# Reordering a product, a routing step and two row updates at the end of an attention and mixture-of-depths kernel

## The chip, the cores and the metric

The kernel runs on one core of one Trainium2 chip. A core has a matrix engine (TensorE, PE in the profile), a vector engine (VectorE, DVE), an engine for copies and functions (ScalarE, ACT), a general engine (GpSimd, POOL), an engine that here issues transfers only (SyncE, SP) and 16 DMA engines. [...] The metric is device time in microseconds; the time of the kernel before is 681.06 us, the median of three runs that lie between 681.03 and 681.25 us.

## What is computed

Attention with pooled queries runs over 8 batches, 8 heads, 1152 keys and 64 channels. Its output, 576 rows of 512 channels a batch, goes through a mixture-of-depths layer that updates 128 rows of every batch.

```python
q_pool = q.reshape(B, H, S // 2, 2, D).mean(axis=3)
attn = softmax(q_pool @ k.transpose(0, 1, 3, 2) / sqrt(D))
x = (attn @ v), as [B, 576, 512]
for b in range(B):
    scores = x[b] @ w_gate
    top_idx = the 128 rows with the highest scores
    xe = x[b, top_idx]
    h = np.maximum(xe @ w1, 0.0)          # 512 -> 1024
    ye = h @ w2                           # 1024 -> 512
    g = 1.0 / (1.0 + np.exp(-scores[top_idx]))
    out[b, top_idx] = xe + g[:, None] * ye     # all other rows stay x
```

## The kernel before, in words

**The main loop.** `run` goes over 64 halves: 32 pairs of heads, each in two halves of 288 pooled queries. A half is scores on TensorE, exponents on ScalarE, their sums on GpSimd and VectorE, and the weighted values on TensorE. All rows of a finished batch go to the output in memory; the picked rows are later read back, updated and written over.

**The layer for picked rows.** Two batches are taken together. Both weight layers are done by a scheme with seven products of half-size blocks in place of eight: the input blocks a11, a12 (first batch) and a21, a22 (second batch), four sums s1 to s4 of them, and weight blocks b11, b21, b22 and sums t1 to t4 of the weights. The seven products are, in the numbering of `second_layer`, (a11, b11), (a12, b21), (s1, t1), (s2, t2), (s3, t3), (s4, b22), (a22, t4). Their results are added up to the blocks of the output. `product` is one of them: 16 passes of TensorE over 128 columns in the first layer (line 1434), 8 passes over 256 columns in the second (line 1444). It takes its PSUM tile from `banks`, a pool of four tiles that are handed out in rotation, so that the tile of one call has to be free of what was put into it four calls earlier.

**The ending.** Batches 4 and 5 (their second layer), and 6 and 7 (both layers), are left for `ending`, which starts when the last half has been computed. Nothing schedules here: the order of the Python calls is the order of the instructions on every engine. The layers are generators, and `pieces(unit, n)` runs one up to its n-th `yield`. The units are: `layer`, the first layer of batches 4 and 5; `second`, the products of a second layer, in a given order, one at a `next`; `third`, the first layer of batches 6 and 7; `new`, the routing of batch 7.

**Routing of batch 7** (`routed`, b = 7). VectorE counts, for each row, how many rows score higher (line 1125), and makes from the ranks five 0/1 matrices (the picks, line 1167; a `yield` follows). Five small products with these (line 1177, ten passes) give the picked rows' numbers and gates; ScalarE copies them out (1185; a `yield`). A transposition (1188) turns them into columns, ScalarE copies these (1189, 1190), and GpSimd gathers the rows with an indirect DMA into the tile named `lines` (1223; a `yield`). Later, TensorE transposes the gathered rows (1271), ScalarE copies them (1272), and they are the input of `third`'s remaining products.

**The stretch that the change touches** is this (lines 1584 to 1594). ScalarE copies the result of `third`'s first product; the rest of the ranking and the picks; the five small products and their copy; product 7 of batches 4 and 5 and its copy to y7 (1587); the transposition and the gather; what is left of `layer`, which is one addition on VectorE and the ReLU of block c21 on ScalarE (1469); the four sums of the second layer's inputs on VectorE (1521), for products 3 to 6; `third`'s second product (a12, b21) with its addition on VectorE and its ReLU on ScalarE (`hidden`, 1467); then products 3, 4 and 5 of batches 4 and 5.

**The last rows.** At the end come the seven products of batches 6 and 7 in the order 1, 7, 3, 4, 5, 6, 2. `scaled` (1448) is one VectorE operation that adds gate times a block to half of the rows of a batch. Product 5 is part of both halves of batch 7's rows, so two operations add it (1637, 1638); then GpSimd writes the rows of batch 7 (1639), and, after products 6 and 2, those of batch 6 (1642). The rows of batch 7 are in the tile `lines`, those of batch 6 in `xe`. The write of batch 6 waits until the write of batch 7 has landed.

Of the kernel before, what the change touches and what calls it, by code (L numbers as in the profile page):

```python
# [539 lines left out]
class _Plain:  # L540
# [886 lines left out]
    def product(self, layer, of, by, to):  # L1427

        n = of.shape[1]
        if layer == 1:  # L1430
            to = self.lines_of(to)[:, :, 0 : of.shape[2]]
            for f in range(by.shape[2] // P):
                for k in range(n):
                    self.nc.tensor.matmul(  # L1434
                        to[:, f, :],
                        lhsT=by[:, k, f * P : (f + 1) * P],
                        rhs=of[:, k, :],
                        start=k == 0,
                        stop=k == n - 1,
                    )  # L1440
        else:
            to = to[0 : of.shape[2], 0 : by.shape[2]]
            for k in range(n):
                self.nc.tensor.matmul(to, lhsT=of[:, k, :], rhs=by[:, k, :], start=k == 0, stop=k == n - 1)  # L1444
        return to
# [9 lines left out]
    def first_layer(self, a, s, c, m, kept=None):  # L1455

        copy = self.nc.scalar.copy
        (a11, a12, _, a22), (s1, s2, s3, s4), (c11, c12, c21, c22), (u, w) = a, s, c, m  # L1460
        b11, b21, b22 = (self.quarter(1, i, j) for i, j in ((0, 0), (1, 0), (1, 1)))
        t1, t2, t3, t4 = (self.summed(1, i) for i in range(4))

        def product(of, by):
            return self.product(1, of, by, self.banks()[:, 0, :])

        def hidden(to, x, y):
            self.add(to, x, y)
            self.nc.scalar.activation(to, to, AF.Relu)

        copy(u, product(a11, b11))
        yield
        hidden(c11, u, product(a12, b21))
        yield
        copy(w, product(s1, t1))
        yield
        self.add(u, u, product(s2, t2))
        self.add(w, w, u)
        yield
        ps = product(s3, t3)  # L1480
        hidden(c22, w, ps)
        self.add(u, u, ps)
        yield
        hidden(c12, w, product(s4, b22))
        yield
        ps = product(a22, t4)
        if kept is not None:
            copy(kept, ps)
            yield
            ps = kept  # L1490
        hidden(c21, u, ps)
        yield
# [30 lines left out]
    def ending(self, halves, old):  # L1523


        nc, half, copy, add = self.nc, self.Dm // 2, self.nc.scalar.copy, self.add
        last = halves[-1]["pair"]

        def pieces(unit, n=None):
            for i, _ in enumerate(unit):  # L1530
                if i + 1 == n:
                    break

        tokens, a, s = self.left
        w = tokens[0]["w"]
# [5 lines left out]
        layer = self.first_layer(a, s, c, m, kept)  # L1541
# [13 lines left out]
        _, new, _ = self.routing.pop()  # L1555
        pieces(old, 1)
        pieces(new, 1)
        pieces(layer, 2)
        for of in (halves[-3]["pair"], last):
            self.divided(of)  # L1560
            self.stored(of)
# [7 lines left out]
        y1, y2, y7, y3, y4 = (acc[1][0:w, i * half : (i + 1) * half] for i in range(5))  # L1569
        room = self.ffn.tile([P, 4, 512], F32, name="s", bufs=1).rearrange("p a n -> p (a n)")  # L1570
        s = self.lines_in(room, self.NFC // 2, w, 4)
        second = self.second_layer(c, s, (1, 2, 7, 3, 4, 5, 6))
# [4 lines left out]
        n = self.NFC * P  # L1577
# [4 lines left out]
        sums = self.lines_in(room[:, 2 * n :], self.ND // 2, w, 4)  # L1582
        third = self.first_layer(a, sums, of_tiles, self.lines_in(self.room[:, 6 * half :], 4, w, 2))
        pieces(third, 1)

        pieces(new, 2)
        copy(y7, next(second))
        pieces(new, 1)
        pieces(layer)
        self.four_sums(c, s)  # L1590
        pieces(third, 1)
        to = [token["xe"][0:w, i * half : (i + 1) * half] for token in tokens for i in range(2)]
        four, five = tokens
# [6 lines left out]
        ps = next(second)  # L1600
# [4 lines left out]
        ps = next(second)  # L1605
# [13 lines left out]
        six, seven = tokens = self.last_tokens  # L1619
        to = [token["xe"][0:w, i * half : (i + 1) * half] for token in tokens for i in range(2)]  # L1620
        y1, y7, y3, y4 = (self.room[0:w, i * half : (i + 1) * half] for i in range(6, 10))
# [3 lines left out]
        second = self.second_layer(of_tiles, s, (1, 7, 3, 4, 5, 6, 2))  # L1625
        copy(y1, next(second))
        self.scaled(to[0], y1, six, to[0])
        ps = next(second)
# [3 lines left out]
        self.scaled(to[2], y4, seven, to[2])  # L1632
        self.add(y3, y3, y4)
        self.scaled(to[3], y3, seven, to[3])
        self.scaled(to[1], y3, six, to[1])
        ps = next(second)
        self.scaled(to[3], ps, seven, to[3])
        self.scaled(to[2], ps, seven, to[2])
        self.written(seven, seven["index"])
        self.scaled(to[1], next(second), six, to[1])  # L1640
        self.scaled(to[0], next(second), six, to[0])
        self.written(six, six["index"])
# [190 lines left out]
```

## Time and profile before

| | us |
|---|---|
| median of three runs | 681.06 (681.03 to 681.25) |
| the profiled execution | 682.7 |
| its span, first to last instruction | 680.9 |
| TensorE busy | 671.4 (99%) |
| VectorE busy | 573.9 (84%) |
| GpSimd busy | 504.0 (74%) |
| ScalarE busy | 453.9 (67%) |
| DMA, mean over the span | 150 GB/s |

The granted TensorE clock is 0.999 of full speed. Times in the text that have two digits behind the point and lie between 600 and 681 are moments in the span of the profiled execution. In a timeline line the columns are the start, the duration from the first start to the last end, the engine, the line of the kernel, the operation, what it writes and reads, the number of instructions, and in brackets how long the engine sat idle before and what ended that. A matrix multiplication of the program appears as two passes in the profile: x16 on line 1434 is one whole product of a first layer, x8 on line 1444 one of a second layer. [...] the time until the data has landed is in the list of DMA issues.

### The profile page before, as it was taken

To read this page: it belongs to the slowest core of one execution; us is meant where nothing else is said; L and a number is where in the kernel's file an instruction comes from. 1 tells how busy PE (TensorE), PEld (TensorE's weight loads), DVE (VectorE), ACT (ScalarE), POOL (GpSimd) and SP (SyncE) were. 2 spreads that over 40 slices of the span, in tenths; PEclk is the share of its full clock that TensorE was granted. 3 is DMA by queue.
4 is the path that set the end of the run, shared out by engine and by line. 5 is a ranking of instruction groups with operands and counts; after the bars stand their busy time and mean duration, and the time that the engine had idled before them with its cause. 6 is when DMAs were issued, how large, how long until landed. Compare 5 with 4: busy or idle time off the path is not lost.

```text
span 680.9 us, 23432 instructions
## 1 busy us (share of the span) xinstructions
PE 671.4 (99%) x9954; PEld 445.8 (65%) x9954; DVE 573.9 (84%) x816; ACT 453.9 (67%) x990; POOL 504.0 (74%) x476
## 2 busy tenths in 40 slices
PE   8999999999999999999999999999999999999996
PEld 6656666665666568676666657767666665658895
DVE  3878998999999887686998987686999998798774
ACT  5677777777877773856777778483787777773220
POOL 4778888889888983866897888383889889885011
PEclk9999999999999999999999999999999999999999
DMA  8888899858886785753879688674588878735310
GB/s 165 165 180 185 199 195 198 165 104 190 193 187 125 166 164 93 205 96 75 206 150 203 125 177 161 128 179 80 118 208 188 151 159 163 173 100 134 63 41 36
DMA packets 391786, 101.99 MB, mean 150 GB/s; under 512 B 371577, under 2 KB 375545, under 8 KB 390649
## 3 DMA queue, kind: packets, MB, share of 16 engines
q1 hardware_dynamic: 390232, 96.03, 67.8%
q0 software_dynamic: 1280, 4.20, 1.9%
q8 instruction: 79, 1.29, 0.7%
q14 instruction: 35, 0.28, 0.2%
q10 hardware_dynamic: 160, 0.20, 0.1%
HBM read 82.77 MB, written 17.62 MB: 147 GB/s over the span
## 4 chain that ended last, share of the span: by engine, by line
PE 85%; DVE 7%; issue 3%; DMA 2%; POOL 1%; ACT 1%; SPq 0%; DVEq 0%; POOLq 0%; ACTq 0%
PE ps L882 38%; PE ps L900 37%; PE ps L1357 7%; DVE fold L926 2%; DVE pick L1125 2%; PE ps L1444 1%; ACT p L889 1%; DMA lines<-row_rank 1%; POOL acc L921 1%; DMA p<-in_q_dram 1%; DVE acc L1453 0%; DMA out_dram<-xe,index 0%; DMA out_dram<-lines,index 0%; DVE kT L778 0%; PE ps L1434 0%
## 5 line engine op out<-in xcount | busy, mean ns | idle before, releaser
L889 ACT ACTIVATE p<-ps 128x576 f32<-128x576 f32 x576 | 320.8, 696 | 3.0 <-PE ps L882 2.8
L921 POOL TENSOR_TENSOR acc<-p 128x576 f32<-128x576 f32 x192 | 278.7, 1479 | 29.2 <-ACT p L889 28.9
L882 PE MATMUL ps<-qT,kT 64*64 64x288 f32 x4608 | 293.0, 404 | 0.7 <-DVE token L632 0.5
L900 PE MATMUL ps<-p,v_sb 64*64 64x288 f32 x4608 | 291.3, 403 | 0.0
L882 PEld LDWEIGHTS ps<-qT,kT 64*64 64x64 f32 x4608 | 172.8, 132 | 108.5 <-ACT p L889 18.8
L900 PEld LDWEIGHTS ps<-p,v_sb 64*64 64x64 f32 x4608 | 172.6, 133 | 107.0 <-ACT p L889 14.0
L926 DVE TRANSPOSE_TENSOR_REDUCE fold<-p 128x54 f32<-128x1728 f32 x64 | 126.2, 1972 | 31.7 <-ACT p L889 31.2
L926 DVE TRANSPOSE_TENSOR_REDUCE fold<-acc 128x54 f32<-128x1728 f32 x64 | 124.6, 1947 | 10.9 <-POOL acc L921 10.6
L908 ACT COPY two<-ps 128x576 f32<-128x576 f32 x64 | 40.8, 638 | 136.5 <-PE ps L900 130.3
L910 POOL TENSOR_TENSOR av<-two 128x288 f32<-128x288 f32 x64 | 51.8, 809 | 69.9 <-ACT two L908 69.8
L778 DVE STREAM_TRANSPOSE kT<-kb 128x1152 f32<-128x1152 f32 x31 | 73.6, 2373 | 0.0
L989 POOL TENSOR_TENSOR prod<-avb,w_gate 128x288 f32<-128x288 f32 x64 | 52.0, 814 | 1.2 <-DVE red L1047 1.0
L1125 DVE TENSOR_SCALAR_CACHE_REDUCE pick<-line 128x127 f32<-128x127 f32 (+4 forms) x80 | 45.2, 565 | 4.4 <-DMA line<-gate_lines 2.2
L775 POOL TENSOR_TENSOR qp<-qb 128x576 f32<-128x576 f32 x31 | 43.7, 1409 | 3.8 <-DMA qb<-in_q_dram 3.8
L979 DVE STREAM_TRANSPOSE avb<-av 128x288 f32<-128x288 f32 x64 | 28.6, 447 | 18.5 <-POOL av L910 18.5
L966 ACT ACTIVATE sums<-total,tiny 32x18 f32<-32x18 f32 x124 | 38.2, 308 | 1.9
L1025 POOL TENSOR_TENSOR x<-avb,rec 128x576 f32<-128x576 f32 x30 | 34.8, 1161 | 0.0
L951 ACT COPY groups<-sum 32x36 f32<-32x36 f32 x124 | 27.2, 219 | 2.9 <-DVE sum L936 1.4
L1047 DVE TENSOR_REDUCE red<-prod 128x9 f32<-128x288 f32 x64 | 27.9, 435 | 0.1
L936 DVE TENSOR_REDUCE sum<-fold 128x18 f32<-128x108 f32 x64 | 21.9, 342 | 2.2
L782 DVE STREAM_TRANSPOSE qT<-qp 128x576 f32<-128x576 f32 x31 | 23.2, 747 | 0.0
L1196 DVE SCALAR_TENSOR_TENSOR pick<-lines,token,token_line 128x640 f32<-128x640 f32 x7 | 18.1, 2587 | 3.4 <-DMA lines<-row_rank 3.3
(168 smaller groups left out, 437.3 us busy)
## 6 DMA issues: line engine op xcount, KB each, us to landing
kb<-in_k_dram SPq DMA_DIRECT2D x124, 144.0 KB, 4.0
qb<-in_q_dram SPq DMA_DIRECT2D x124, 144.0 KB, 4.4
v_sb<-in_v_dram SPq DMA_DIRECT2D x31, 576.0 KB, 5.6
out_dram<-x SPq DMA_DIRECT2D x128, 72.0 KB, 4.8
tw<-tw SPq DMA_DIRECT2D x8, 1024.0 KB
lines<-row_rank SPq DMA_DIRECT2D x7, 640.0 KB
w<-in_moe_w_dram SPq DMA_DIRECT2D x8, 512.0 KB
tw<-tw SPq DMA_DIRECT2D x8, 512.0 KB, 4.0
```

Source lines behind the costliest of these rows:

```text
L775: nc.gpsimd.tensor_tensor(out=qp[:, :, :], in0=pair["q"][:, :, 0, :], in1=pair["q"][:, :, 1, :], op=ALU.add)
L778: nc.vector.transpose(kT.rearrange("p (c i g) -> p c g i", c=self.NC, i=BLK), pair["k"].rearrange("p (g c) d -> p c g d", c=self.NC),)
L882: nc.tensor.matmul(sc[keys, j, 0:n], lhsT=pair["kT"][rows, c * P + keys.start : c * P + keys.stop], rhs=pair["qT"][rows, qs], start=True, ...
L889: nc.scalar.activation(p[:, c // G, c % G, :, :], sc[:, :, 0:n], AF.Exp, scale=self.scale)
L900: nc.tensor.matmul(av[j * self.D : (j + 1) * self.D, e, 0:n], lhsT=half["pair"]["v"][keys, j, c, :], rhs=half["p"][keys, c // G, c % G, j, :],
L908: nc.scalar.copy(two[:, :, :], av[:, :, 0:n])
L910: nc.gpsimd.tensor_tensor(out=half["av"][:, :], in0=two[:, 0, :], in1=two[:, 1, :], op=ALU.add)
L921: nc.gpsimd.tensor_tensor(out=acc[:, u, :], in0=units[:, 0, u, :], in1=units[:, 1, u, :], op=ALU.add)
L926: nc.vector.tensor_reduce(fold[:, a, :], of.rearrange("p u (m d) -> p (u m) d", d=BLK), AX.X, ALU.add, apply_transpose=True,)
L989: self.nc.gpsimd.tensor_tensor(out=pair["prod"][:, ns, :], in0=pair["avb"][:, ns, :], in1=self.w_gate[:, hp : hp + 1, :].broadcast_to([P, ...
L1125: nc.vector.tensor_scalar(out=cmp[0:rows, 0 : part.stop - part.start], in0=near[0:rows, part], scalar1=sc[0:rows, t : t + 1], scalar2=None ...
L1357: nc.tensor.matmul(args[0], lhsT=args[1], rhs=args[2], start=k == 0, stop=k == n - 1)
```

## The change

The generator `first_layer` gets a `yield` between its second product and what is done with it, so that the product's TensorE work and its VectorE and ScalarE work can be called for at different places. In `ending`, product 7 of batches 4 and 5 and its copy are called before the picks; the small products with the picks come behind the ReLU of c21 and the four sums, and the second product of `third` between them and the transposition. At the end, the two operations that add product 5 to batch 7's rows become one that reads the product twice, and it and the write of batch 7 come before the second update of batch 6.

```diff
 def first_layer(self, a, s, c, m, kept=None):
         copy(u, product(a11, b11))
         yield
-        hidden(c11, u, product(a12, b21))
+        ps = product(a12, b21)
+        yield
+        hidden(c11, u, ps)
         yield
 def ending(self, halves, old):
-        pieces(layer, 2)
+        pieces(layer, 3)
...
         pieces(third, 1)
-
-        pieces(new, 2)
         copy(y7, next(second))
+
         pieces(new, 1)
         pieces(layer)
         self.four_sums(c, s)
+        pieces(new, 1)
+        pieces(third, 1)
+        pieces(new, 1)
         pieces(third, 1)
...
         self.scaled(to[3], y3, seven, to[3])
+        ps = next(second)
+        self.scaled(
+            seven["xe"][0:w, :].rearrange("p (i n) -> p i n", i=2),
+            ps.unsqueeze(1).broadcast_to([w, 2, half]),
+            seven,
+            seven["xe"][0:w, :].rearrange("p (i n) -> p i n", i=2),
+        )
+        self.written(seven, seven["index"])
         self.scaled(to[1], y3, six, to[1])
-        ps = next(second)
-        self.scaled(to[3], ps, seven, to[3])
-        self.scaled(to[2], ps, seven, to[2])
-        self.written(seven, seven["index"])
         self.scaled(to[1], next(second), six, to[1])
```

## The prediction

> **What bounds the kernel now.** I read the page first. Its busy times name the engine:
>
> ```profile
> PE 671.4 (99%) x9954; PEld 445.8 (65%) x9954; DVE 573.9 (84%) x816; ACT 453.9 (67%) x990; POOL 504.0 (74%) x476
> ```
>
> TensorE is busy all but 9.5 us, and the chain that ended last is 85% TensorE. So an edit is worth what it takes from TensorE's idle time or work, and whatever follows TensorE's last pass. The diff touches only the ending, so next I read its timeline on TensorE:
>
> ```profile
> 637.10 1.95 PE L1434 MATMUL ps<-p,w 128*128 128x128 f32 x16
> 640.34 1.34 PE L1177 MATMUL ps<-pick,meta 128*2 128x128 f32 x10 [1.29 <-DVE pick L1167]
> 641.61 1.99 PE L1444 MATMUL ps<-kT,hT 128*128 128x256 f32 x8
> 643.54 0.22 PE L1188 MATMUL ps<-ident,pick 2*128 2x2 f32 x1
> 643.69 2.05 PE L1434 MATMUL ps<-p,w 128*128 128x128 f32 x16
> 645.57 1.89 PE L1444 MATMUL ps<-kb,s 128*128 128x256 f32 x8
> ...
> 650.76 0.63 PE L1271 MATMUL ps<-ident,lines 128*128 128x128 f32 x4
> ...
> 652.95 5.52 PE L1434 MATMUL ps<-p,tw 128*128 128x128 f32 x48
> ```
>
> The rows are: third's first product; the wait for the picks with its 1.29 us of idleness; product 7 (its weights lie in kT); the transposition; third's second product; product 3; the transposes of the gathered rows; and third's next three products. After the one bracket TensorE has no idle entry until its end. Then the timelines of VectorE and ScalarE around the bracket:
>
> ```profile
> 639.91 1.06 DVE L1167 TENSOR_SCALAR pick<-token_line,rank 128x128 f32<-128x128 f32 x5
> 640.90 0.68 DVE L1453 TENSOR_TENSOR hT<-acc 128x512 f32<-128x512 f32 x1
> 644.70 0.69 DVE L1521 TENSOR_TENSOR s<-hT 128x512 f32<-128x512 f32 x1 [3.13 <-ACT hT L1469]
> ```
>
> ```profile
> 643.64 0.37 ACT L1587 COPY acc<-ps 128x256 f32<-128x256 f32 x1 [1.67 <-PE ps L1444]
> ...
> 644.01 0.65 ACT L1469 ACTIVATE hT<-hT 128x512 f32<-128x512 f32 x1
> ```
>
> The input of c21's ReLU is ready at 641.58, but the ReLU stands on ScalarE behind the copy of product 7, and VectorE sits 3.13 us for it. Product 3 needs the first of those sums, and is reached with little to spare (645.39 against 645.57). Last, the end of the timeline of all engines, and the gather and batch 7's write in the list of DMA issues (the last number is us to landing):
>
> ```profile
> 671.03 0.48 DVE L1448 SCALAR_TENSOR_TENSOR xe<-p,own_gate,xe 128x256 f32<-128x256 f32 x1
> 671.42 0.87 DVE L1448 SCALAR_TENSOR_TENSOR lines<-ps,own_gate,lines 128x256 f32<-128x256 f32 x2
> 672.57 0.98 POOL L1299 DMA_INDIRECT out_dram<-lines,index  x1 [12.41 <-DVE lines L1448]
> 672.76 0.48 DVE L1448 SCALAR_TENSOR_TENSOR xe<-ps,own_gate,xe 128x256 f32<-128x256 f32 x1 [0.47 <-PE ps L1444]
> 674.49 0.48 DVE L1448 SCALAR_TENSOR_TENSOR xe<-ps,own_gate,xe 128x256 f32<-128x256 f32 x1 [1.24 <-PE ps L1444]
> 676.06 0.98 POOL L1299 DMA_INDIRECT out_dram<-xe,index  x1 [2.51 <-DMA out_dram<-lines,index]
> ```
>
> ```profile
> lines<-out_dram,index POOLq DMA_INDIRECT x1, 3.4
> out_dram<-lines,index POOLq DMA_INDIRECT x1, 2.7
> ```
>
> Batch 6's rows are ready at 674.97, but their write starts at 676.06, released by the landing of batch 7's write (672.57 + 2.72 = 675.29, by the chain). So the end follows batch 7's write, not TensorE's last pass.
>
> **What the Trainium skill says.** "Perfetto Trace Analysis", section "Summary: the profiler window per engine type": the end of a TensorE instruction is only estimated. So I count from start to start: a first-layer product takes 660.41 to 662.20 = 1.79 us, so the idle stretch is 640.34 − (637.10 + 1.79) = 1.45 us, not 1.29. "VectorE: DVE Perf Modes", section "The TRN2 errata", gives VectorE a fixed cost and one cycle of 0.96 GHz for each fp32 element without a faster mode, and a PSUM source a larger fixed cost. The first agrees: a tensor addition over 256 takes 0.42 us and over 512 0.68, 0.26 apart for 256/0.96 = 0.267. The second is not seen: the updates from PSUM take 478 ns, from SBUF 485. "DMA: Bandwidth & Descriptors", section "Anatomy of one DMA", gives a fixed 2.0 us and bytes at 436 GB/s; for the 256 KB of a batch's rows my estimate from it is 2.6 us, the trace has 2.7.
>
> **The change part by part.** Nothing is added to or taken from TensorE, ScalarE or GpSimd; VectorE has one instruction fewer. All moments are of the profiled execution (own time 682.7, of which 1.8 lie around its span of 680.9); it is 1.64 us above the median, and as the edits act inside the span, what they take off it I take off the median too.
>
> *Product 7 into the idle stretch.* It starts at 638.89 instead of 641.61. Its weights landed at 610.8 + 7.2 = 618.0, its input, c22, comes from a ReLU that ended at 632.80. Its PSUM tile is the one that held the kept product, copied out by 634.73. It takes 1.73 (647.30 to 649.03), to 640.62. The picks: the first is ready at 640.21, the fifth at 640.97, while the small products take 0.25 us each; so they no longer wait and end at 640.62 + 1.27 = 641.89. Third's second product follows; its tile was freed by a copy that ended at 637.67. Counted by the sequence before, from 640.34 to 645.57 lie 5.23 us of the same four items with their changes of shape, none removed, only permuted. So product 3 can start at 638.89 + 5.23 = 644.12 instead of 645.57: **1.45 us**. Bounds: the page's own idle figure, 1.29; and 1.60, if a 0.15 us loss between items of different shape (product 7 took 1.93 behind the small products, 1.73 elsewhere) occurs once less.
>
> *Does product 3 have its input?* The copy of product 7 stands ahead of the ReLU, and ends near 641.2; VectorE's addition still ends at 641.58. The ReLU runs 641.6 to 642.25, the first sum 642.3 to 643.0, all four end at 642.3 + 2.54 = 644.85. 1.1 us to spare, more than before. The copy of the small products is now queued behind that ReLU: 642.25 to 642.5, while the transposition that needs it is reached at 643.97. Third's addition and ReLU come at 644.85 and 645.5, and behind them ScalarE's copy of product 3, ready at 645.9; no cost, the cover being products 4 and 5 on TensorE.
>
> *The gather is put behind third's second product.* The transposition moves from 643.54 to 643.97, so the gather's issue from 644.35 to at most 644.78 (its two ScalarE copies no longer stand behind product 7's copy). GpSimd has nothing queued before it, SP no transfer there. With 3.4 us it lands at 648.2. Its consumers, the transposes, are now reached 1.45 earlier, at 649.31. Slack falls from 3.0 to 1.1 us; price 0. If it landed as late as the slowest of the eight gathers in this trace (6.0 us, one in the loop beside its loads), TensorE would wait to 650.8.
>
> *From there to the end* all shifts together. The closest point is the sums for third's next product: ready at 652.50, used at 652.95; their chain (transposes, copy, sums) starts from the same TensorE moment, and VectorE ahead of it is free at 649.2, before 650.6. The writes of batches 4 and 5, the check on the sums and the last products move along.
>
> *Batch 7's last update.* Before, product 5 was added in two operations, 671.42 to 672.29, behind batch 6's update at 671.03. Now one operation over 512 elements follows the update that ends at 671.10. It reads what that one wrote, so it starts where dependent ones did (0.03 us after the end): 671.13, and product 5 is there (669.11 + 1.89 = 671.00). Its duration is not in the trace. Low bound 0.739 × 512/576 = 0.66, from VectorE's broadcast multiplication over 576; I take 0.478 + 256/0.96 = 0.745; high bound, by the skill's fixed costs (an estimate: 62 cycles more from PSUM), 0.81, or no merging gain at all, 0.87. It ends at 671.88, not 672.29: **0.41 us** earlier (0.28 to 0.50). The write starts 0.28 later as before, at 672.16, lands at 674.88, and batch 6's write starts 0.77 behind that, at 675.65. Its own rows would allow 674.97 + 0.28 = 675.25, so the whole 0.41 reaches the end, and up to 0.81 would have. Batch 6's update, now behind, ends at 672.3, before product 6 is there (672.76); its cover is 0.47 us.
>
> Sum: 1.45 + 0.41 = 1.86. Span 680.9 − 1.86 = 679.04; time 681.06 − 1.86 = **679.20 us**, −0.27%.
>
> **The rivals.** *Head only, 679.6.* The wide operation reads PSUM twice over a repeated dimension and could take 1.16 us, the point at which batch 7's write starts as before. For: no row has this form. Against: the broadcast over 576 runs at 0.74. *Gather late, about 680.7.* At 6.0 us it eats the 1.45 and leaves 0.41. For: slack of only 1.1 us. Against: at this place it took 3.4, the least of the eight, and no other transfer runs beside it; the change brings none. *The idle stretch stays, 680.65.* If product 7 waited for a PSUM tile or its weights it would stand in front of the picks and fill nothing. Against: both were ready over 4 us earlier. *Slower:* the gather is the one edge that was moved later while its reader moved earlier. From a landing time of 4.5 us it costs, from 6.4 (650.76 + 0.41 − 644.78) the kernel is slower than before, and over 0.2% slower from 7.8 us: at 8.5 us, 681.06 + 2.1 = 683.2. Only the order against it speaks, no landing in the trace is above 6.0.
>
> **How the numbers follow.** A difference of 0.2% is 1.36 us, about what a measurement of this kernel can tell from no change; faster means below 679.70, slower above 682.42. Full gain 0.70, spread by the bounds (1.29 to 1.60 and 0.28 to 0.50) over 678.9 to 679.5, all faster but for 0.02; head only 0.13, on both sides of the line, 0.08 faster; late gather 0.08 and idle stretch 0.03, both within 0.2%; slower 0.06. That is 0.76 faster, 0.18 the same, 0.06 slower. The range holds the full gain, head only and the start of the late gathers: 678.6 to 680.3; the lower end adds 0.3 to the bounds for what a different build does elsewhere.
>
> **What would show it.** In the profile after: no idle entry before the small products, product 7 starting near 638.9, product 3 near 644.1, the transposes of the gathered rows near 649.3 without a wait, gather issue near 644.7; VectorE's wait for the ReLU down from 3.1 to about 0.7; one update of 512 elements with about 0.75 us; batch 7's write starting 1.9 us earlier at 670.7 and batch 6's still released by its landing. The prediction is wrong if the transposes wait for the gather, if product 3 waits for the sums, or if the wide update takes over 1 us.

## The result and the profile after

The changed kernel takes 679.24 us, the median of 13 runs (678.84 to 679.98), beside 680.93 us for the kernel before (13 runs, 680.38 to 681.25). The ratio is 0.9976, with a 95% interval of 0.9969 to 0.9983: 1.69 us less, where 1.86 were forecast. That 679.24 lies only 0.04 us from the forecast time of 679.20 is luck: the gain came out 0.17 us smaller, and the kernel before was measured 0.13 us faster here than the 681.06 from which the forecast was counted.

The page's busy times of the changed kernel:

```profile
PE 669.3 (99%) x9954; PEld 447.3 (66%) x9954; DVE 576.5 (85%) x815; ACT 453.3 (67%) x990; POOL 503.8 (74%) x476
```

VectorE has its one instruction fewer. The span of this execution is 677.4 us, 3.5 below that of before, and 1.88 of that lie ahead of the edited stretch: third's first product starts at 635.22 here and at 637.10 before, behind the same code. In the ten profiles of this study that start lies anywhere from 635.22 to 638.77. So spans are not compared below. The measure is the time from the start of that product to the start of batch 6's write, which takes in all edits: 676.06 − 637.10 = 38.96 us before, 672.48 − 635.22 = 37.26 us after, 1.70 apart, as the medians are.

The timeline of TensorE in the changed kernel, by the columns explained above:

```profile
635.22 1.95 PE L1434 MATMUL ps<-p,w 128*128 128x128 f32 x16
637.00 1.89 PE L1444 MATMUL ps<-kT,hT 128*128 128x256 f32 x8
638.83 1.34 PE L1177 MATMUL ps<-pick,meta 128*2 128x128 f32 x10
640.10 2.05 PE L1434 MATMUL ps<-p,w 128*128 128x128 f32 x16
642.08 0.22 PE L1188 MATMUL ps<-ident,pick 2*128 2x2 f32 x1
642.23 1.99 PE L1444 MATMUL ps<-kb,s 128*128 128x256 f32 x8
644.06 1.89 PE L1444 MATMUL ps<-qb,s 128*128 128x256 f32 x8
...
647.51 0.63 PE L1271 MATMUL ps<-ident,lines 128*128 128x128 f32 x4
```

The bracket with the idle time is gone. Product 7 follows third's first product at once, and product 3 starts 7.01 us after that product (8.47 before), the transposes of the gathered rows 12.29 us after it (13.66 before), without a wait. VectorE's wait for the ReLU of c21 shrank from 3.13 to 0.70 us, in its timeline:

```profile
640.35 0.69 DVE L1523 TENSOR_TENSOR s<-hT 128x512 f32<-128x512 f32 x1 [0.70 <-ACT hT L1469]
```

The gather starts at 642.77 and, by the list of DMA issues, lands after 3.6 us, at 646.37, 1.14 us before its readers:

```profile
lines<-out_dram,index POOLq DMA_INDIRECT x1, 3.6
```

The end, in the timeline of all engines and then in the chain that ended last (start, duration, what):

```profile
665.86 1.89 PE L1444 MATMUL ps<-kb,p 128*128 128x256 f32 x8
...
667.38 0.48 DVE L1448 SCALAR_TENSOR_TENSOR lines<-p,own_gate,lines 128x256 f32<-128x256 f32 x1
...
667.97 0.75 DVE L1448 SCALAR_TENSOR_TENSOR lines<-ps,own_gate,lines 128x512 f32<-128x512 f32 x1
...
668.99 0.97 POOL L1299 DMA_INDIRECT out_dram<-lines,index  x1 [12.06 <-DVE lines L1448]
...
671.25 0.48 DVE L1448 SCALAR_TENSOR_TENSOR xe<-ps,own_gate,xe 128x256 f32<-128x256 f32 x1 [1.24 <-PE ps L1444]
672.48 0.97 POOL L1299 DMA_INDIRECT out_dram<-xe,index  x1 [2.51 <-DVE xe L1448]
```

```profile
668.99 2.72 DMA out_dram<-lines,index
...
671.75 0.51 issue
```

The wide update takes 0.75 us, and batch 7's write starts 3.13 us after product 5 (3.46 before). GpSimd's line for it lasts 0.97 us, but by the chain its data has landed only 2.72 us after the start of that line. Batch 6's write still follows the landing of batch 7's: 3.49 us lie between the two starts, as before the change. The bracket of the last timeline line names VectorE's update of `xe` as its releaser, but that update ends at 671.73, 0.75 us earlier, while a write that really waits for VectorE starts 0.28 us behind it (667.97 + 0.75 = 668.72, to 668.99). Here the chain, which goes back to the landing at 671.71, has it right.

### The profile page after: what moved, and what is told of

It reads as the page before. It is cut to its first block, busy times and chain, and to the rows that moved or that the text cites. A ratio compares the mean times of both kernels' runs of the same rounds, so it can differ in the third digit from the quotient of the medians.

```text
span 677.4 us, 23431 instructions
## 1 busy us (share of the span) xinstructions
PE 669.3 (99%) x9954; PEld 447.3 (66%) x9954; DVE 576.5 (85%) x815; ACT 453.3 (67%) x990; POOL 503.8 (74%) x476
## 4 chain that ended last, share of the span: by engine, by line
PE 95%; issue 2%; DMA 1%; DVE 1%; POOL 0%; SPq 0%; ACT 0%; POOLq 0%; DVEq 0%
PE ps L882 41%; PE ps L900 41%; PE ps L1357 7%; PE ps L1434 2%; PE ps L1444 2%; DMA p<-in_q_dram 1%; DMA out_dram<-xe,index 0%; DMA out_dram<-lines,index 0%; DVE p L1523 0%; DVE pick L1659 0%; DVE p L1453 0%; DVE xe L1448 0%; PE ps L1177 0%; DVE acc L1453 0%; POOL out_dram L1299 0%
```

## The experiments

All times below are counted from the start of third's first product in the profile of the kernel named. The ratios are to the kernel before timed beside each: 680.93 us for the result, 682.48 us for "head only" to "product 7 alone" (one chip), 682.26 us for "changed, again" and the last three (another chip). So medians are compared only with those taken beside them.

| kernel | product 3 | transposes | batch 7's write | batch 6's write | ratio to before (95%) |
|---|---|---|---|---|---|
| before | 8.47 | 13.66 | 35.47 | 38.96 | |
| changed | 7.01 | 12.29 | 33.77 | 37.26 | 0.9976 (0.9969 to 0.9983) |
| changed, again | 7.01 | 12.29 | 33.77 | 37.26 | 0.9977 (0.9967 to 0.9987) |
| head only | 7.01 | 12.29 | 34.10 | 37.59 | 0.9983 (0.9976 to 0.9990) |
| tail only | 8.46 | 13.64 | 35.12 | 38.62 | 0.9995 (0.9987 to 1.0003) |
| two updates first | 7.01 | 12.30 | 33.90 | 37.40 | 0.9981 (0.9975 to 0.9988) |
| product 7 alone | 7.33 | 12.51 | 33.99 | 37.49 | 0.9977 (0.9970 to 0.9985) |
| gather behind product 3 | 6.77 | 13.29 | 34.86 | 38.36 | 0.9993 (0.9986 to 1.0000) |
| no last update of 7 | 7.01 | 12.29 | 32.92 | 36.79 | 0.9968 (0.9956 to 0.9980) |
| product 3 last | 7.01 | 12.29 | 33.33 | 36.82 | 0.9969 (0.9958 to 0.9980) |

**The changed kernel again.** It was profiled and timed once more, beside the last three.

> The changed kernel itself, on the same chip as the three others, to compare them with. Theory: 37.26 us from third's first product to batch 6's write, as in its first profile, and a ratio to before of 0.9976 within its interval. Rival (the interval itself varies from execution to execution): it differs by over 0.1 us.

The interval came out at 37.26 us both times. In the six profiles whose kernels have the changed head, product 3 starts at 7.01 us in every one and the transposes at 12.29 or 12.30. So differences of a tenth of a microsecond can be read.

**The two halves of the change.** First the head alone:

```diff
-        ps = next(second)
-        self.scaled(<both halves of batch 7's rows>, <ps, twice>, seven, ...)
-        self.written(seven, seven["index"])
         self.scaled(to[1], y3, six, to[1])
+        ps = next(second)
+        self.scaled(to[3], ps, seven, to[3])
+        self.scaled(to[2], ps, seven, to[2])
+        self.written(seven, seven["index"])
```

> The new order of product 7, the small products and third's second product, with batch 7's last two updates as before. Theory (the filled idle stretch is worth 1.46 us up to product 3, of which the change of shape between transposition and product 3 takes 0.1 back, and the tail is worth 0.33 by itself): from the start of third's first product to batch 6's write 37.6 us (38.96 before, 37.26 in the changed kernel), median 1.35 us below before, about 679.6. Rival (the gain before the picks seen in the two profiles, 1.88 us, comes from the new order too): the time is over 2.5 us below before.

Then the tail alone, the same edit the other way round on the kernel before:

> Only batch 7's one wide update and its place ahead of batch 6's update; the head as before. Theory: batch 7's write starts 0.33 us earlier counted from the start of product 5, batch 6's write follows its landing as before, the interval from third's first product to batch 6's write is 38.6 us (38.96 before), median 0.3 us below before, about 680.6. Rival (the end follows TensorE's last product and batch 6's rows): no difference in the interval.

The head alone gave 37.59 us and a median 1.33 us below before; the tail alone 38.62 us and 0.28 us below, an amount that the times cannot tell from none (the interval reaches 1.0003) but the trace can. 1.37 and 0.34 add up to 1.71, the change is 1.70: the halves don't interact. The timeline of the tail alone, of all engines, shows where its part comes from (product 5, then batch 7's write):

```profile
669.02 1.89 PE L1444 MATMUL ps<-kb,p 128*128 128x256 f32 x8
...
672.15 0.98 POOL L1299 DMA_INDIRECT out_dram<-lines,index  x1 [12.06 <-DVE lines L1448]
```

Batch 7's write starts 3.13 us after product 5, as in the changed kernel. The rival for the head, that the 1.88 us ahead of the edits come from the new order too, falls: the median is 1.33 us below before and not over 2.5, and third's first product started at 636.92 with the same head, and at 636.19 in the second profile of the changed kernel itself.

**Merging or place?** The changed kernel with two updates of 256 elements in the new place:

```diff
         ps = next(second)
-        self.scaled(<both halves of batch 7's rows>, <ps, twice>, seven, ...)
+        self.scaled(to[3], ps, seven, to[3])
+        self.scaled(to[2], ps, seven, to[2])
         self.written(seven, seven["index"])
```

> The changed kernel, but product 5 is added to batch 7's rows by two updates over 256, ahead of batch 6's update. It tells the merging of the two operations from their new place. Theory (two take 0.87 us, one takes 0.75): batch 7's write starts 0.12 us later than in the changed kernel, counted from the start of product 5 (3.13 there, 3.25 here); so the merging gives about a third of the tail's gain and the place two thirds. Rival (all of it is the merging): the write starts 3.45 us after product 5, as before the change.

In VectorE's timeline of this kernel, followed by GpSimd's (product 5 started at 667.31):

```profile
669.41 0.87 DVE L1448 SCALAR_TENSOR_TENSOR lines<-ps,own_gate,lines 128x256 f32<-128x256 f32 x2
```

```profile
670.56 0.98 POOL L1299 DMA_INDIRECT out_dram<-lines,index  x1 [12.19 <-DVE lines L1448]
```

3.25 us after product 5, between 3.13 and 3.46: the new place is worth 0.21 us, the merging 0.12. So the place ahead of batch 6's update did more than the merging. The wait of 2.10 us from the product's start to the first update is that of the wide update (2.11), so the width or the repeated reading doesn't cause it.

**Product 7 alone.** Only the line with product 7 is moved ahead of the picks:

```diff
         copy(y7, next(second))
-
+        pieces(new, 2)
         pieces(new, 1)
         pieces(layer)
         self.four_sums(c, s)
-        pieces(new, 1)
-        pieces(third, 1)
-        pieces(new, 1)
-        pieces(third, 1)
+        pieces(third, 2)
```

> The changed kernel, but only product 7 is moved: third's second product is again behind the transposition, and the copy of the small products and the index copies stand again ahead of the ReLU of c21 on ScalarE. Theory: TensorE now waits between the small products and the transposition for ScalarE's copy, about 0.4 us, so product 3 starts 7.4 us after third's first product (7.01 in the changed kernel, 8.47 before); median 0.4 us above the changed kernel, about 679.65. Rival (product 7 alone is enough, the other moves are idle): 7.0 us and no difference from the changed kernel.

TensorE's timeline of this kernel:

```profile
640.18 1.34 PE L1177 MATMUL ps<-pick,meta 128*2 128x128 f32 x10
641.87 0.22 PE L1188 MATMUL ps<-ident,pick 2*128 2x2 f32 x1 [0.35 <-ACT pick L1185]
642.02 2.05 PE L1434 MATMUL ps<-p,w 128*128 128x128 f32 x16
643.91 1.89 PE L1444 MATMUL ps<-kb,s 128*128 128x256 f32 x8
645.64 1.89 PE L1444 MATMUL ps<-qb,s 128*128 128x256 f32 x8
```

TensorE waits for ScalarE's copy between the small products and the transposition, as expected: from the one's start to the other's it takes 1.69 us here and 1.27 in the changed kernel, where third's second product fills this wait. Product 3 starts 0.32 us later than in the changed kernel, but the end is only 0.23 later, a little over half of the 0.4 that was expected: third's second product takes 1.89 us here and 1.98 in the changed kernel, product 3 itself 1.73 and 1.83 (see below). The times, 0.9977, don't resolve the 0.23. The order has another side: here the gather starts 5.98 us after third's first product, 1.57 earlier than in the changed kernel, and lands after 3.5, about 3 us before its readers. So the other moves buy 0.23 us with nearly 2 us of the gather's cover.

**How much cover has the gather?** In the changed kernel, the transposition, the index copies and the gather are moved behind product 3:

```diff
         self.four_sums(c, s)
         pieces(new, 1)
-        pieces(third, 1)
-        pieces(new, 1)
-        pieces(third, 1)
+        pieces(third, 2)
...
         copy(y3, next(second))
+        pieces(new, 1)
         self.add(y2, y2, y1)
```

> The changed kernel with the transposition, the index copies and the gather behind product 3 instead of ahead of it. It measures the slack of the gather. In the changed kernel the gather is issued 4.74 us before its readers, the transposes, and lands after 3.6: slack 1.14. Theory (1.14 us is all the cover): the gather starts about 2.3 us later (1.7 for product 3, the rest for two ScalarE jobs now ahead of the index copies), so TensorE waits about 1.2 us for it in front of the transposes, and the end is 1.2 us later than in the changed kernel, about as much as the head gained. Rival (the readers have more cover than the trace's landing time tells): no wait, no difference.

The timeline of all engines:

```profile
648.45 1.10 POOL L1223 DMA_INDIRECT lines<-out_dram,index  x1 [13.60 <-ACT own_gate L1190]
...
652.06 0.72 PE L1271 MATMUL ps<-ident,lines 128*128 128x128 f32 x4 [0.83 <-DMA lines<-out_dram,index]
```

The gather started 9.68 us after third's first product (7.55 in the changed kernel), TensorE waited for its landing, the transposes started 1.00 us later than in the changed kernel, and the end came 1.10 us later. The forecast of the slack, 1.1 us, was right, and there is no further cover behind it: a gather 2.1 us later gives back most of what the whole change brought.

**How far does the end follow batch 7's write?** The wide update is left out:

```diff
         ps = next(second)
-        self.scaled(<both halves of batch 7's rows>, <ps, twice>, seven, ...)
         self.written(seven, seven["index"])
```

> The changed kernel without the wide update that adds product 5 to batch 7's rows (the product itself is still computed); so batch 7's rows are written without it. It measures how far the end follows batch 7's write. Theory (batch 6's write starts 0.77 us behind the landing of batch 7's write, or 0.28 us behind its own rows, whichever is later): batch 7's write starts 0.86 us earlier, but batch 6's only 0.45 to 0.5 earlier than in the changed kernel (36.8 us after third's first product, there 37.26), since its own rows are not ready before. Rival 1 (the end follows the landing alone): 0.86 earlier. Rival 2 (the end follows TensorE alone): no difference.

The timeline of all engines:

```profile
670.10 0.97 POOL L1299 DMA_INDIRECT out_dram<-lines,index  x1 [11.23 <-DVE lines L1448]
...
673.21 0.48 DVE L1448 SCALAR_TENSOR_TENSOR xe<-ps,own_gate,xe 128x256 f32<-128x256 f32 x1 [1.24 <-PE ps L1444]
673.97 0.97 POOL L1299 DMA_INDIRECT out_dram<-xe,index  x1 [2.89 <-DVE xe L1448]
```

Batch 7's write started 0.85 us earlier than in the changed kernel, batch 6's only 0.47. The two writes are now 3.87 us apart instead of 3.49, and the second starts 0.28 us behind its own rows (673.69 to 673.97): here it is VectorE and, ahead of it, TensorE that set the end. (The chain of this profile still goes back to the landing, at 672.82, which is 1.15 us ahead of the write; in this run the bracket has it right.) So a still earlier write of batch 7 can take another 0.47 us off the changed kernel, and no more as long as batch 6's rows are ready no earlier.

**Taking it.** The last products are put in another order, with product 3, which belongs to only one half of batch 7's rows, as the last that batch 7 needs (`four_sums` takes the order of its sums as an argument):

```diff
-        self.four_sums(of_tiles, s)
+        self.four_sums(of_tiles, s, (2, 0, 1, 3))     # the sum for product 5 first
...
-        second = self.second_layer(of_tiles, s, (1, 7, 3, 4, 5, 6, 2))
+        second = self.second_layer(of_tiles, s, (1, 7, 5, 4, 3, 6, 2))
         copy(y1, next(second))
         self.scaled(to[0], y1, six, to[0])
-        ps = next(second)
-        self.scaled(to[2], ps, seven, to[2])
-        copy(y3, next(second))
-        self.add(y4, y1, next(second))
-        self.scaled(to[2], y4, seven, to[2])
-        self.add(y3, y3, y4)
-        self.scaled(to[3], y3, seven, to[3])
-        ps = next(second)
-        self.scaled(<both halves of batch 7's rows>, <ps, twice>, seven, ...)
+        self.scaled(to[2], next(second), seven, to[2])
+        self.add(y3, y1, next(second))
+        four = next(second)
+        self.add(y3, y3, four)
+        self.scaled(<both halves of batch 7's rows>, <y3, twice>, seven, ...)
+        ps = next(second)
+        self.scaled(to[3], ps, seven, to[3])
         self.written(seven, seven["index"])
-        self.scaled(to[1], y3, six, to[1])
+        self.add(y4, y1, four)
+        self.add(y4, y4, ps)
+        self.scaled(to[1], y4, six, to[1])
```

> The changed kernel with the last products in the order 1, 7, 5, 4, 3, 6, 2, the wide update used for the sum of products 1, 5 and 4, and product 3, which belongs to one half of batch 7's rows only, as the last one for them. Theory: batch 7's last update is one of 256 elements that starts as soon as product 3 is there, so its write starts 0.44 us earlier (33.3 us after third's first product, in the changed kernel 33.77) and lands as batch 6's own rows become ready; the end is 0.44 us earlier, 36.8 in place of 37.26; the median lies below the changed kernel by about 0.4 us. Rival (product 5 as the third waits for its sum, or VectorE is late with the longer sums): TensorE idles between products 7 and 5 and the gain is lost.

The timeline of all engines:

```profile
667.78 1.89 PE L1444 MATMUL ps<-kb,p 128*128 128x256 f32 x8
...
668.44 0.75 DVE L1448 SCALAR_TENSOR_TENSOR lines<-p,own_gate,lines 128x512 f32<-128x512 f32 x1
...
669.71 0.48 DVE L1448 SCALAR_TENSOR_TENSOR lines<-ps,own_gate,lines 128x256 f32<-128x256 f32 x1 [0.52 <-PE ps L1444]
...
670.47 0.98 POOL L1299 DMA_INDIRECT out_dram<-lines,index  x1 [11.64 <-DVE lines L1448]
...
673.96 0.98 POOL L1299 DMA_INDIRECT out_dram<-xe,index  x1 [2.51 <-DVE xe L1448]
```

The wide update now runs ahead of the product that is waited for, batch 7's write starts 2.69 us after that product (in the changed kernel 3.13 us after product 5), and batch 6's write at 36.82, 0.44 us earlier than in the changed kernel, as worked out. TensorE shows no idle time. The median is 680.19 us beside 680.47 for the changed kernel timed beside it and 682.26 before; the 0.28 between the first two lies within the intervals of the ratios, so that it is faster than the changed kernel rests on the trace.

## Why the prediction was right

**Product 7 into the idle stretch: right, 1.37 us kept of 1.45.** Counted from third's first product, product 3 came 1.46 us earlier, as worked out. But the same four items, only permuted, do not take the same time to the transposes. A product takes 0.1 us longer for each short item (the small products or the transposition) next to it. Before, product 7 stood between two of them and took 1.93 us (4.51 to 6.44), third's second product behind one 1.88, product 3 its plain 1.73. After, they take 1.83, 1.98 and 1.83: one such border more, since the one between third's first product and the small products falls into the idle stretch there and costs nothing. The step that I wrote as "none removed, only permuted" missed that; the extra 0.1 falls inside product 3, behind the moment at which I stopped counting. My upper bound of 1.60 had the sign of this wrong too: it let one such loss fall away, and one was added.

**ScalarE, the sums and the PSUM tiles: right.** The first sum started 5.13 us after third's first product, forecast 5.2, and no wait came in the place of the one removed. "Product 7 alone" shows what the other moves are for: they are worth 0.23 us.

**The gather at a price of 0: right, and close.** Forecast were an issue at 7.68 us at most, 3.4 us to landing and 1.1 us of slack; measured 7.55, 3.6 and 1.14. In all ten profiles the gather landed after 3.4 to 3.6 us, so the late landing of the rival occurred in none; that a late gather costs what was worked out is shown by the run that starts it 2.1 us later. One reading was wrong: that no landing in the trace is above 6.0 us holds for the gathers only, since the load of product 7's weights, by the prediction's own figure, took 7.2.

**Batch 7's last update: direction and mechanism right, 0.33 us for 0.41.** The duration was forecast as 0.745 us from the slope of VectorE's rows, and measured as 0.75. The term that was mis-sized is its start: I took 0.03 us behind the update it depends on; it was 0.11 (667.86 to 667.97). The two narrow updates in the same place started with the same 0.11, so neither width nor repeated reading is the reason. In "product 3 last" the wide update reads a sum in SBUF in place of a product in PSUM: it takes 0.75 us there too, but starts 0.04 us behind the operation it depends on. The later start was seen only where the update reads a product of TensorE that has just become readable. The wide and the narrow updates of product 5 wait for TensorE's product and for the update ahead at nearly the same moment (other results of TensorE were read 1.93 us after a product's start, which puts product 5 at 667.79); how these two waits make up the 0.11 was not separated. That the whole gain of the tail reaches the end, up to a second bound, was right: that bound was forecast at 0.81 − 0.41 = 0.40 us behind the change and found at 0.47.

**The sum.** 1.37 + 0.33 = 1.70 in the trace, 1.69 in the medians, 1.86 forecast. The difference between the two profiled spans, 3.5 us, would have misled: half of it lies ahead of the edits.

## What to carry to other kernels

Fill a wait of the bounding engine with work that is ready, and then check what was moved behind that work, and what is now read earlier: here the gather's cover fell from 3.0 us to 1.14, mostly because its readers came 1.37 us earlier and only 0.30 because it starts later itself, and a further step took most of the gain back. Where the last transfer of a kernel waits for the landing of the one ahead, the end follows the first of them; what the last operations before the first transfer cost, and in which order they stand, matters more than what the second one needs, until the second one's own data becomes the bound. And measure a short edit between two points in the trace that enclose it, not by the spans of two executions.

## What the runs showed of the hardware that was not expected

- Next to the small products (weights of 2 columns) or the transposition of 2 rows, a product on TensorE takes 0.1 us longer on each side: 1.73 us plain, 1.83 with one such neighbour, 1.93 between two (8 passes over 256 columns); 1.79, 1.88 and 1.98 for 16 passes over 128 columns. The four transposes of 128x128 cost their neighbours nothing: the products on both sides take 1.73 us in the profile before (649.03 to 650.76, 651.22 to 652.95). Why the narrow items cost this is not shown.
- At the end of this kernel, GpSimd starts the indirect write of batch 6 0.77 us behind the landing of the one it waits for (3.49 less 2.72), but an indirect write 0.28 us behind a VectorE result that it waits for. The trace may name the wrong releaser for such a write, in the bracket (the changed kernel) or in the chain ("no last update of 7"); the distance tells which it was.
